# Moving a load of queries behind the first loop turn, and reordering the start, in an attention and ReGLU kernel

## The chip, the cores and the metric

The kernel runs on one core of a Trainium2 chip. The metric is the time of one execution on the device, in microseconds (us), given as the median of several executions with the lowest and the highest. The "span" of a profile is the time from the first to the last instruction of the profiled execution; here it is about 2 us shorter than the device time of the same execution. PE is TensorE, PEld its weight load, DVE is VectorE, ACT is ScalarE, POOL is GpSimd and SP is SyncE.

## The reference

```python
def _attn_ref(q, kv, w_sr):                       # q (4, 12288, 128), kv (4, 384, 32, 128)
    kv_pool = kv.reshape(B, H // 4, 4, W // 4, 4, C).mean(axis=(2, 4))
    k = v = kv_pool.reshape(B, -1, C) @ w_sr      # 768 keys of 128; keys and values are the same
    s = (q @ k.transpose(0, 2, 1)) / np.sqrt(C)
    a = np.exp(s - s.max(-1, keepdims=True))
    a /= a.sum(-1, keepdims=True) + 1e-09
    return a @ v

def _moe_ref(x, w_gate, w_val, w_out):            # x (49152, 128), weights 128 x 1536 and 1536 x 128
    return (np.maximum(x @ w_gate, 0.0) * (x @ w_val)) @ w_out
```

The output of the attention, seen as 49,152 rows, is the input of the second function. Input and output are in 32-bit floats; the kernel computes most matmuls in 16 bits.

## The kernel before

The kernel works on tiles of 512 query rows; four tiles are a group, whose queries are loaded and transposed together. One turn of the main loop has twelve steps. In each step TensorE does the value, gate and output projections of one 128-wide block of the feed-forward part for an earlier tile, and one twelfth of the attention of a later tile. Ahead of the loop stands a hand-ordered start: it loads the first image lines, pools and projects the 768 keys of the first batch, and does the attention of the first three tiles. All engines run in exactly the order in which the code issues instructions (`manual_schedule`), so moving a line in the source moves an instruction on its engine.

The parts that the change and the argument touch, with cuts marked:

```python
def q_load(g):                      # one group of queries: 512 KB of fp16, cast on the way, GpSimd's queue
    ...
    q16 = work.tile([128, GRP * NS, C], FP16, tag="q16", bufs=2)
    nc.gpsimd.dma_start(q16, q[b, n0 : n0 + GRP * T, :].rearrange("(p s) c -> p s c", p=128))

def q_turn(g):                      # its transposing DMA, on SyncE's queue
    ...
    nc.sync.dma_start_transpose(qT, q16.rearrange("p s c -> p (s c)"))

def block_move(kvT, blocks, i, j):  # 16 of these carry one pair of key chunks of a later batch
    rows, columns = slice(32 * i, 32 * (i + 1)), slice(32 * j, 32 * (j + 1))
    nc.sync.dma_start(kvT[columns, :, rows], blocks[rows, :, columns])
# ... cut ...
kv_load(0, 0, between=lambda: q_load_plain(0, 2))   # four image lines; queries after line 1
q_load_plain(2, GRP)
for pair in range(1, NJC // 2):
    kv_load(0, pair)                                # eight more image lines
# ... cut ...
def fill(n):                                        # matmuls that only keep TensorE's clock up
    for _ in range(n):
        nc.tensor.matmul(idle, ident16, filler, start=True, stop=True)
fill(8)
# ... cut: attention on image pairs 0 and 1 ...
scores_of(0, 1)
turn_values(0, 1)
s2 = add_lines(2)                                   # sum of two image lines, on VectorE
nc.vector.tensor_tensor(s2, s2, line(2, 2), op=ALU.add)
s1 = add_pixels(s2)
scores_of(1, 1)
# ... cut ...
gate = const.tile([128, 1], FP32)
nc.gpsimd.tensor_copy(gate, line(2, 2)[:, 0, 0, 0:1])   # holds GpSimd's loads back until line 2 is there
for own in (slice(0, D_FF // 2), slice(D_FF // 2, D_FF)):
    nc.gpsimd.dma_start(wv16[:, own], moe_w_val[:, own])
    nc.gpsimd.dma_start(wg16[:, own], moe_w_gate[:, own])
q_load(1)
q_turn(1)
nc.gpsimd.dma_start(wo16, moe_w_out.rearrange("(fb f) c -> f fb c", f=128))
q_load(2)
# ... cut: pair 2, the end of the start ...
for k in range(LAG, last + 1):
    g, ph = divmod(k, GRP)
    if ph == 1:
        q_turn(g + 1)
        q_load(g + 2)
    for step in range(NFB):
        # ... cut: out_proj(kO, step), value_proj(kF, step), scores or values of tile k, x_turn ...
        if kF < NT:
            gate_proj(kF, step)
```

The softmax here doesn't subtract the row's maximum and nothing guards it: scores larger than these inputs give would overflow.

## Time and profile before

| | before |
|---|---|
| device time, median of 3 (lowest to highest) | 1044.61 us (1044.28 to 1045.14) |
| span of the profile | 1042.5 us |
| TensorE busy | 1032.8 us, 99% |
| first value projection of the loop starts | 29.80 us |
| 14th value projection starts | 41.68 us |
| last value projection starts | 1035.48 us |

The page, the stretches and the chain of waits are shown in the prediction below.

### The profile page before, as it was taken

The page shows a single profiled execution, that of the slowest core. Times are in us where ns is not written, and L with a number is a line of the kernel's source. Part 1 is how long each engine was busy: PE and PEld are TensorE (multiplying, and loading weights), DVE is VectorE, ACT ScalarE, POOL GpSimd, SP SyncE. Part 2 cuts the span into 40 slices and gives each one's busy share as a digit, 9 for nine tenths or more (in the row PEclk, how much of TensorE's full clock was granted, in tenths as well). Part 3 has the DMA queues.
Part 4 walks back from the last instruction along what each step waited for, and adds up shares of the span by engine and source line. Part 5 has one row for each costly group of instructions (what it writes and reads, how often), then busy time and mean ns, then how long its engine had stood idle before and what let it go on. Part 6 is the DMA issues. An engine that isn't in the chain of part 4 may idle for free.

```text
span 1042.5 us, 26058 instructions
## 1 busy us (share of the span) xinstructions
PE 1032.8 (99%) x9928; PEld 684.6 (66%) x9928; DVE 911.9 (87%) x1669; ACT 909.5 (87%) x1749; POOL 107.0 (10%) x127
## 2 busy tenths in 40 slices
PE   8999999999999999999999999999999999999998
PEld 5566666666666666666666666666666666666665
DVE  3788889898988888998888888999888888888898
ACT  4888888888888888888888888888888888888887
POOL 2000045100000006400000003440000000000000
PEclk9999999999999999999999999999999999999999
DMA  8833254432322335534234134561531422212111
GB/s 300 129 76 76 78 178 137 96 76 52 87 53 66 72 124 141 150 79 80 61 58 87 31 87 132 150 159 41 92 80 39 73 63 55 67 31 67 32 47 47
DMA packets 140253, 92.53 MB, mean 89 GB/s; under 512 B 117728, under 2 KB 118624, under 8 KB 140128
## 3 DMA queue, kind: packets, MB, share of 16 engines
q1 hardware_dynamic: 134544, 77.56, 28.5%
q0 software_dynamic: 5440, 13.24, 7.7%
q8 instruction: 77, 1.26, 0.5%
q14 instruction: 48, 0.39, 0.1%
q10 hardware_dynamic: 144, 0.07, 0.0%
HBM read 52.76 MB, written 25.17 MB: 75 GB/s over the span
## 4 chain that ended last, share of the span: by engine, by line
PE 95%; DMA 4%; POOL 0%; SPq 0%; issue 0%; DVE 0%
PE bank_ps L285 25%; PE bank_ps L264 24%; PE bank_ps L275 24%; PE bank_ps L226 12%; PE bank_ps L215 11%; DMA parts<-in_kv_dram 2%; DMA qT<-q 1%; DMA q<-in_q_dram 1%; PE bank_ps L179 0%; DMA xT<-x 0%; SPq L128 0%; POOL wv L440 0%; POOL wg L441 0%; POOL gate L438 0%; SPq L93 0%
## 5 line engine op out<-in xcount | busy, mean ns | idle before, releaser
L278 DVE SCALAR_TENSOR_TENSOR hT<-bank_ps,val 128x512 f16<-128x512 f32 x1152 | 759.9, 686 | 101.2 <-ACT val L268 74.8
L268 ACT CAST val<-bank_ps 128x512 f16<-128x512 f32 x1152 | 677.9, 590 | 111.7 <-PE bank_ps L264 109.7
L285 PEld LDWEIGHTS <-hT 128*128 128x128 f16 x4608 | 353.2, 98 | 203.4 <-issue 0.2
L285 PE MATMUL bank_ps<-wo,hT 128*128 128x128 f16 x4608 | 443.6, 219 | 0.0
L264 PE MATMUL bank_ps<-xT,wv 128*128 128x512 f16 x1152 | 436.7, 379 | 0.2 <-DMA xT<-x 0.2
L275 PE MATMUL bank_ps<-xT,wg 128*128 128x512 f16 x1152 | 436.6, 379 | 0.0
L216 ACT ACTIVATE aT<-bank_ps 128x512 f16<-128x512 f32 x576 | 345.4, 604 | 1.4 <-PE bank_ps L215 1.3
L226 PE MATMUL bank_ps<-kv,aT 128*128 128x129 f16 x2304 | 223.5, 220 | 0.1
L226 PEld LDWEIGHTS <-aT 128*128 128x128 f16 x2304 | 177.2, 98 | 68.1 <-issue 0.6
L215 PE MATMUL bank_ps<-qT,kv 128*128 128x512 f16 x576 | 216.9, 379 | 2.6 <-DMA qT<-q 2.2
L275 PEld LDWEIGHTS <-wg 128*128 128x128 f16 x1152 | 112.7, 98 | 65.6
L264 PEld LDWEIGHTS <-wv 128*128 128x128 f16 x1152 | 112.7, 98 | 0.8 <-DMA xT<-x 0.4
L242 DVE TENSOR_TENSOR x<-bank_ps,rinv 128x256 f16<-128x256 f32 x188 | 79.7, 424 | 6.7
L78 POOL DMA_DIRECT2D q<-in_q_dram x23 | 12.5, 543 | 567.3 <-DMA qT<-q 567.2
L303 DVE TENSOR_SCALAR o_sb<-bank_ps 128x512 f32<-128x512 f32 (+1 forms) x95 | 64.0, 674 | 1.3 <-PE bank_ps L285 1.3
L139 POOL TENSOR_TENSOR s<-parts 128x512 f32<-128x512 f32 x36 | 45.3, 1269 | 163.4 <-DMA parts<-in_kv_dram 161.0
L215 PEld LDWEIGHTS <-kv 128*128 128x128 f16 x576 | 56.1, 98 | 5.2 <-DMA qT<-q 2.5
L234 DVE RECIPROCAL rinv<-bank_ps 128x2 f32<-128x2 f32 x192 | 30.6, 160 | 0.6 <-PE bank_ps L226 0.6
L141 POOL TENSOR_TENSOR s<-s 128x512 f32<-128x512 f32 x18 | 22.8, 1267 | 1.4
L143 POOL TENSOR_TENSOR c<-s 128x256 f32<-128x256 f32 x18 | 13.1, 726 | 1.4
L164 ACT COPY kvT<-bank_ps 128x128 f32<-128x128 f32 x4 | 1.1, 265 | 11.6 <-PE bank_ps L153 10.8
L146 POOL TENSOR_TENSOR kv_s<-c 128x128 f32<-128x128 f32 x18 | 8.2, 454 | 1.4
(46 smaller groups left out, 72.1 us busy)
## 6 DMA issues: line engine op xcount, KB each, us to landing
parts<-in_kv_dram SPq DMA_DIRECT2D x48, 512.0 KB, 6.5
out_dram<-o_sb SPq DMA_DIRECT2D x95, 256.0 KB, 2.1
q<-in_q_dram POOLq DMA_DIRECT2D x23, 512.0 KB, 5.2
kvT<-blocks SPq DMA_DIRECT2D x144, 8.0 KB, 1.8
xT<-x SPq DMA_TRANSPOSE x94, 2.5
q<-in_q_dram SPq DMA_DIRECT2D x2, 512.0 KB, 7.2
wv<-in_moe_w_val_dram POOLq DMA_DIRECT2D x2, 192.0 KB, 4.6
wg<-in_moe_w_gate_dram POOLq DMA_DIRECT2D x2, 192.0 KB, 5.0
```

Source lines behind the costliest of these rows:

```text
L139: eng.tensor_tensor(s2[:, i], parts[:, 2 * i, h], parts[:, 2 * i + 1, h], op=ALU.add)
L215: nc.tensor.matmul(s_ps, kv16[:, k // NST, jc, 0:C], qT_of(k), start=True, stop=True)
L216: nc.scalar.activation(aTs[k][:, jc, :], s_ps, AF.Exp, scale=qk_scale)
L226: nc.tensor.matmul(x_ps[:, i, :], aTs[k][:, jc, s * 128 : (s + 1) * 128], kv16[:, k // NST, jc, C : 2 * C + 1], start=(jc == 0 and i == 0) ...
L234: nc.vector.reciprocal(rinvs[k, half], x_banks[k, half][:, :, C : C + 1])
L242: nc.vector.tensor_tensor(x16s[k][:, 2 * half : 2 * half + 2, :], x_ps[:, :, 0:C], rinv.to_broadcast([128, 2, C]), op=ALU.mult,)
L264: nc.tensor.matmul(va_ps, wv16[:, fb * 128 : (fb + 1) * 128], xTs[k], start=True, stop=True)
L268: nc.scalar.copy(val, va_ps)
L275: nc.tensor.matmul(g_ps, wg16[:, fb * 128 : (fb + 1) * 128], xTs[k], start=True, stop=True)
L278: nc.vector.scalar_tensor_tensor(hTs[k][:, fb, :], g_ps, 0.0, vals.pop((k, fb)), op0=ALU.max, op1=ALU.mult)
L285: nc.tensor.matmul(o_ps, hTs[k][:, fb, s * 128 : (s + 1) * 128], wo16[:, fb, :], start=first, stop=(fb == NFB - 1), skip_group_check=True,)
L303: nc.vector.tensor_scalar(o_sb, o_ps, 1.0 / X_SCALE**2, None, op0=ALU.mult)
```

## The change

The intent is a shorter start. The load of the third group of queries (`q_load(2)`) leaves the place where it runs beside the transposing DMA of the second group, and goes behind the last activation of the first loop turn. The first queries are loaded behind the whole first image pair. The cast of the second tile's queries goes to ScalarE, so that two casts run side by side. The scores of three tiles come before the values' transposes of pair 1, the sum of the lines of pair 2 moves ahead of them, and four fillers go.

```diff
-    def q_cast(i):
+    def q_cast(i, engine=nc.vector):
         q16 = work.tile([128, NS, C], FP16, tag="q16s", bufs=3, name="q16s")
-        nc.vector.tensor_copy(q16, q32s[i])
+        if engine is nc.scalar:
+            nc.scalar.copy(q16, q32s[i])
+        else:
+            nc.vector.tensor_copy(q16, q32s[i])
 ... cut: kv_load loses its argument "between" ...
-    kv_load(0, 0, between=lambda: q_load_plain(0, 2))
-    q_load_plain(2, GRP)
+    kv_load(0, 0)
+    for i in range(0, GRP, 2):
+        q_load_plain(i, i + 2)
 ...
-    for i in range(2):
-        q_cast(i)
     for dh in range(3):
         for h in range(2):
             turn_add(h, line(0, dh, h), first=dh == 0)
-        if dh == 1:
-            fill(3)
-            q_turn_pe(0)
-            q_turn_pe(1)
-            fill(1)
 ...
         project_chunk(h, (nc.vector, nc.scalar)[h])
+    for i in range(2):
+        q_cast(i, (nc.vector, nc.scalar)[i])
+        q_turn_pe(i)
+    scores_of(0, 0)
+    scores_of(1, 0)
     for i in range(2, GRP):
         q_cast(i)
-    scores_of(0, 0)
-    scores_of(1, 0)
     q_turn_pe(2)
+    turn_values(0, 0)
     q_turn_pe(3)
-    turn_values(0, 0)
 ...
-    scores_of(0, 1)
+    s2 = add_lines(2)
+    for k in range(GRP - 1):
+        scores_of(k, 1)
     turn_values(0, 1)
-    s2 = add_lines(2)
     nc.vector.tensor_tensor(s2, s2, line(2, 2), op=ALU.add)
     s1 = add_pixels(s2)
-    scores_of(1, 1)
-    scores(2, 2)
     attend(0, 1)
-    scores(2, 3)
     scores_of(3, 1)
 ...
     nc.gpsimd.dma_start(wo16, moe_w_out.rearrange("(fb f) c -> f fb c", f=128))
-    q_load(2)
 ...
                 gate_proj(kF, step)
+            if k == LAG and step == NFB - 1:
+                nc.gpsimd.tensor_copy(gate, hTs[kF][:, step, 0:1])
+                q_load(2)
```

The source lines shift by the change: line 264 (value projection) becomes 265, 215 (scores) 216, 275 (gate projection) 276, 268 (value cast on ScalarE) 269, 216 (exponential) 217, and GpSimd's gate copy goes from 438 to 434.

More of the change, by code (lines that the diff above doesn't have):

```diff
@@ L120, with kv_load @@
     kv_in = {}
-    def kv_load(b, pair, between=None):
+    def kv_load(b, pair):
         parts = work.tile([128, r, 2, r, C], FP32, tag="kv_in", bufs=3)
@@ L128, in kv_load @@
             nc.sync.dma_start(parts[:, dh].rearrange("p h dw c -> p (h dw c)"), rows[dh])
-            if dh == 1 and between is not None:
-                between()
         kv_in[b, pair] = parts
```

## The prediction

> **What bounds the kernel now.** I read the page first: busy time per engine, then the busy tenths by slice.
>
> ```profile
> PE 1032.8 (99%) x9928; PEld 684.6 (66%) x9928; DVE 911.9 (87%) x1669; ACT 909.5 (87%) x1749; POOL 107.0 (10%) x127
> PE   8999999999999999999999999999999999999998
> ```
>
> The reader is to see that TensorE is the bound for the whole span and that only 1042.5 - 1032.8 = 9.7 us of it are idle. The change takes no matmul out of the loop, so it can only win part of these 9.7 us, and 2% would be 20.9 us. Next I asked for the busy time by stretches, to find where the idle time lies (columns: stretch, length, busy time of PE, PEld, DVE, ACT and POOL with counts, granted clock, DMA share, GB/s):
>
> ```profile
> 5.35:13.00 7.65, 6.78 (x49) 4.80 (x49) 2.16 (x7) 0.27 (x1) 0.00 (x0) 1.00 1.02 386
> 13.00:20.00 7.00, 6.82 (x60) 5.09 (x59) 3.39 (x7) 5.20 (x13) 0.00 (x0) 1.00 1.03 412
> 20.00:30.00 10.00, 9.03 (x78) 5.79 (x78) 5.82 (x14) 7.30 (x16) 5.24 (x8) 1.00 0.78 147
> 30.00:40.00 10.00, 8.83 (x76) 5.33 (x74) 9.02 (x20) 9.79 (x24) 0.00 (x0) 1.00 1.29 193
> 40.00:50.00 10.00, 8.99 (x78) 5.57 (x79) 7.15 (x12) 8.59 (x18) 0.53 (x1) 1.00 0.48 72
> 80.00:1030.00 950.00, 949.82 (x9193) 630.70 (x9192) 849.41 (x1550) 843.27 (x1614) 99.38 (x109) 1.00 0.35 83
> ```
>
> From 80 to 1030 us PE is idle for 0.18 us; the rest of the idle time is in the first 42 us and the last 3.6. The largest single hole is around 40 us. The chain of waits, in order of time (start, length, what), says what it is made of:
>
> ```profile
> 11.06 10.21 DMA parts<-in_kv_dram
> 24.43 8.23 DMA q<-in_q_dram
> 32.67 0.02 issue
> 32.68 8.28 DMA qT<-q
> 40.97 0.05 issue
> 41.01 0.39 PE bank_ps L215
> ```
>
> Two things to see. Until about 22.8 us the start follows the image lines as they land back to back (about 1.27 us per 512 KB at some 410 GB/s). Then the second group of queries (q of group 1) lands at 32.67, its transposing DMA lands at 40.97, and PE starts at once. On the timeline the preceding value projection starts at 38.45, so the score matmul was due at 38.45 + 0.22 = 38.67: the hole costs 41.01 - 38.67 = 2.34 us. Last, what ScalarE does around that hole (timeline: start, length, engine, operation, idle before):
>
> ```profile
> 39.02 0.66 ACT L240 ACTIVATE x<-bank_ps,rinv 128x128 f16<-128x128 f32 x2
> 39.53 0.62 ACT L268 CAST val<-bank_ps 128x512 f16<-128x512 f32 x1
> 41.44 0.60 ACT L216 ACTIVATE aT<-bank_ps 128x512 f16<-128x512 f32 x1 [1.28 <-PE bank_ps L215]
> ```
>
> ScalarE comes out of the first loop turn late: it works until 40.15 on what PE finished by 38.8, and is idle for only 1.28 us of the hole.
>
> **What the Trainium skill says.** "DMA: Bandwidth & Descriptors", section "Issuing engines are not separate DMA queues": DMAs of the scalar, sync and gpsimd engines end on the same 16 DMA engines and interleave. The trace agrees: this transpose, beside the loads of wo (lands 34.85) and of the third group (issued 25.97, lands 12.4 us later at 38.37), takes 8.28 us; the same transpose for group 2, at 51.3 us beside one 256 KB store, takes 4.4 us. "TensorE: Matmul & The Clock Gate", Part 1 (The HAM clock gate) has a half clock until the array has been busy for about 3.4 us, and Part 4 (PE-mode transpose) says that transposes do not count as busy in the same way. The trace shows the start: eight fillers take 3.59 us (about 0.43 us each) at 1.7 us, later 128x512 matmuls follow every 0.22 us. Whether the four later fillers keep the clock up is what no run here shows yet. "ScalarE: Activation LUTs", What ACT_TABLE_LOAD costs, gives an ACTIVATE with immediate operands 186 ns + 0.833 ns per column, 613 ns for 512; the trace has 604 for the exponentials.
>
> **The change part by part.**
>
> 1. *Third group's load moved.* Its issue goes from 25.97 us to behind the last activation of the first loop turn (about 40.2 us). So it is gone from the DMA engines while the group 1 transpose runs. Rate under contention: 8.28 us were 5.69 us contended (32.68 to 38.37) plus 2.59 alone; against 4.4 alone that leaves (4.4 - 2.59) / 5.69 = 0.32 of full speed while contended. After the change only wo contends, to 34.85: 2.17 us x 0.32 = 0.69 us of work, the other 3.71 alone, landing at about 32.67 + 2.17 + 3.71 = 38.6, just when PE wants it (38.67). The DMA part of the hole, 2.34 us, should be nearly gone. I do not expect q of group 1 itself to land earlier, since it is ahead of the third group on its queue.
>
> 2. *What ScalarE gives back.* Without the hole ScalarE still has its backlog to 40.02, so its first exponential of this turn moves from 41.44 to 40.02 at best: 1.42 us. In this turn its two steps take 1.52 us (exponentials start at 44.76 and 46.28) and PE's two steps 1.53 (score matmuls at 44.08, 45.60), so it catches up nothing until the next turn, where it first idles (0.19 us every two steps from 52.1). PE can be ahead of it only as far as 8 PSUM banks let it. With a lag of about 1.3 us a value bank is held 1.9 us every 0.76, a score bank 1.9 every 1.53, a gate bank some 2.3 every 0.76, an output bank always: 2.5 + 1.2 + 3.0 + 1 = 7.7 banks, at the edge. I take 1.9 us, between 1.42 (PE fully tied) and 2.34 (not at all).
>
> 3. *First queries behind the whole first image pair.* In the old order image lines 2 and 3 land at 9.78 and 11.04, queries at 8.27 and 12.33. In the new one the lines should land at about 7.9 and 9.3 and the first queries at 11.0. Keys are then ready at about 11.3, but cast, transposes and copy (0.42 + 0.35 + 0.42 with hand-overs) put the first scores at about 12.5 instead of 13.00. That half microsecond ends at the next image lines, which land as before (17.46 for the last of pair 1; the total of bytes ahead is the same): worth about 0.1 us.
>
> 4. *Second cast on ScalarE.* Some 0.5 us (estimated between the 0.42 of DVE and the 0.59 of a value cast) on an engine that waits there: L164 of ScalarE idles 9.6 us before 12.2. It lets two casts run side by side; contained in the 12.5 above.
>
> 5. *Scores of three tiles before the values' turn of pair 1, line sum first.* The 1.22 us sum for pair 2 moves ahead, to 20.0 us. But six score matmuls now stand ahead of the values' transposes; four banks are free, so these wait for the third exponential (20.17 + 3 x 0.51 = 21.7), DVE copies at 22.1 instead of 20.79, and the two sums that follow end at about 24.3 instead of 24.19. PE's transposes of the last line come after eight value matmuls and two scores, at 23.4 instead of 22.9. The serial chain from there to the loop (24.25 to 29.80) moves by about +0.2 us.
>
> 6. *Four fillers gone*: 4 x 0.22 = 0.88 us, all in time when PE waits for lines: 0.
>
> Sum: -1.9 - 0.1 + 0.2 = -1.8 us, plus +0.1 for the clock risk below (20% of a delay, of which the later waits hide most): 1044.6 - 1.7 = **1042.9 us**.
>
> **The rivals.**
>
> *ScalarE takes the place of the DMA.* The hole goes, but PE stalls for banks shortly after. For: ScalarE 9.79 busy of 10 us from 30 to 40, and 5.00 of 5 from 45 to 50. Against: PE ran through the first turn with a lag of 1.1 us. Time: about 1043.2.
>
> *The transpose stays late.* If wo, with its small rows, was the one that slowed it, it lands near 39.5 to 40 and the gain is 1 us or less: 1043.7. For: the transpose and wo overlap from the first moment. Against: the third group overlaps 3.5 us more.
>
> *The clock falls.* From 5.3 to 12.5 us PE now runs nothing but transposes and two small projections. If it drops to half speed, eight scores, the transposes and values before pair 1 take about 2.5 us more than their 3.3, which pushes the start by 1 to 2 us: 1043.5 to 1045. Against: the old stretch had only 4 fillers in 7.6 us and the image lines, not PE, set the pace to 22.8.
>
> *The start gets faster.* If lines land 0.4 us sooner (DMA moved only 320 GB/s in the 6 to 8 us slice, where the queries cut in), all follows: 1042.3.
>
> **Range and chances.** The sure part is 1 to 1.4 us, the full hole plus a better start 2.9. Run to run spread is 0.9 us. So 8 in 10 for 1041.5 to 1044.5. Neither side comes near 20.9 us: 0.98 for within 2%, 0.01 each for the others.
>
> **What would show it.** Step 1 right: the transpose of group 1 takes under 6.5 us and PE's wait for it is under 0.3 us. Step 2 right: ScalarE has no idle of 1 us at 40 us, and PE has waits on ACT or DVE of 0.2 to 0.8 us between 39 and 55. Step 3: first score near 12.5 and pair 1's last line still near 17.5. Step 5: first value projection between 29.6 and 30.2. The clock: score matmuls at 12.5 to 15 us longer than 0.38 us, or spaced 0.43, would show the fall. I would be wrong above all if a new hole of over 1 us appears before 30 us, or if the third group, now issued at the same time as the fourth, delays the transposes behind it on the sync queue so that PE waits at 50 or 60 us.

## More of the kernel before

The value projections are good marks, since each step has one of them: the first shows when the loop starts, the distance from the first to the 14th shows what the first turn and the step after it cost, and the rest is the steady loop. One more view of the kernel before is worth having, TensorE's waits (engine, tile and line, what it waited for, then us in total, times, longest):

```profile
PE bank_ps L215 <- DMA qT<-q: 2.2, 1, 2.2
```

It is the largest wait of TensorE in the whole kernel. The line says that a score matmul (line 215) waited once, for 2.2 us, for the transposed queries.

## The result and the profile after

| | before | after |
|---|---|---|
| device time, median of 6 (lowest to highest) | 1044.88 us (1044.15 to 1046.53) | 1042.90 us (1041.60 to 1043.41) |
| ratio of the means, 95% interval | | 0.9978 (0.9965 to 0.9991) |
| span of the profile | 1042.5 us | 1041.0 us |
| first value projection | 29.80 us | 30.07 us |
| from the first to the 14th | 11.88 us | 9.61 us |
| from the 14th to the last | 993.80 us | 994.33 us |

The change is within 2%, and the median is the one predicted. The last three rows say where the time went: the loop starts 0.27 us later, the first turn is 2.27 us shorter, and 0.53 us is lost later in the loop. The last value projection comes 1.47 us earlier (1035.48 and 1034.01), which is the difference of the spans.

The first line of the page after, busy time by engine:

```profile
PE 1032.3 (99%) x9924; PEld 684.2 (66%) x9924; DVE 911.7 (88%) x1668; ACT 909.8 (87%) x1750; POOL 106.6 (10%) x128
```

Four matmuls fewer are the four fillers; one instruction more on ScalarE is the moved cast, and one more on GpSimd the new gate copy. TensorE's idle time in the span is now 1041.0 - 1032.3 = 8.7 us. The stretches after, with the columns that the prediction explains:

```profile
5.35:13.00 7.65, 6.03 (x45) 4.60 (x46) 1.34 (x4) 1.05 (x3) 0.00 (x0) 1.00 0.97 359
20.00:30.00 10.00, 8.84 (x77) 5.76 (x77) 5.59 (x13) 7.33 (x16) 3.96 (x7) 1.00 0.94 189
30.00:40.00 10.00, 9.94 (x85) 6.08 (x84) 8.97 (x22) 9.52 (x24) 0.00 (x0) 1.00 0.80 118
40.00:50.00 10.00, 10.00 (x90) 6.23 (x89) 8.98 (x15) 10.00 (x21) 1.26 (x3) 1.00 0.67 120
80.00:1030.00 950.00, 949.62 (x9190) 630.22 (x9189) 849.35 (x1551) 843.30 (x1614) 99.53 (x109) 1.00 0.34 83
```

The two rows from 30 to 50 us carry the gain: TensorE was busy for 8.83 and 8.99 us of them before, and is for 9.94 and 10.00 now. The 40 to 50 row has ScalarE busy for all of its 10.00 us and TensorE busy for all of its 10.00 us as well: ScalarE is full, and TensorE does not wait for it. TensorE's timeline around the old hole (start, length, engine, line, operation):

```profile
38.73 0.38 PE L265 MATMUL bank_ps<-xT,wv 128*128 128x512 f16 x1
39.00 0.38 PE L216 MATMUL bank_ps<-qT,kv 128*128 128x512 f16 x1
39.24 0.38 PE L276 MATMUL bank_ps<-xT,wg 128*128 128x512 f16 x1
```

The score matmul that had to wait until 41.01 follows the value projection by 0.27 us. The second group's transposing DMA was issued at 31.92 and landed at 37.92, in 6.00 us where it had taken 8.28. The chain of waits after, up to the start of the loop:

```profile
12.33 11.20 DMA parts<-in_kv_dram
23.67 1.50 PE bank_ps L154 x12
...
29.59 0.44 DVE xT L260
30.07 0.38 PE bank_ps L265
```

The transposing DMA has left the chain. What now leads into the loop is the last image line, then TensorE's transposes of it (line 154) and the chain behind them. In the largest waits of TensorE after, the queries are gone as well, and the image lines have taken the first place among the loads:

```profile
PE bank_ps L154 <- DMA parts<-in_kv_dram: 1.3, 3, 0.6
...
PE bank_ps L265 <- DMA xT<-x: 0.2, 1, 0.2
```

Finally ScalarE's timeline in the first and second loop turns, after:

```profile
39.82 0.63 ACT L269 CAST val<-bank_ps 128x512 f16<-128x512 f32 x1
40.28 0.66 ACT L217 ACTIVATE aT<-bank_ps 128x512 f16<-128x512 f32 x1
...
41.71 0.69 ACT L217 ACTIVATE aT<-bank_ps 128x512 f16<-128x512 f32 x1
...
43.15 0.72 ACT L217 ACTIVATE aT<-bank_ps 128x512 f16<-128x512 f32 x1
```

And the same engine before, after its hole:

```profile
43.23 0.60 ACT L216 ACTIVATE aT<-bank_ps 128x512 f16<-128x512 f32 x1
...
44.76 0.60 ACT L216 ACTIVATE aT<-bank_ps 128x512 f16<-128x512 f32 x1
```

Exponentials come once in two steps. Before, they came 44.76 - 43.23 = 1.53 us apart, after 43.15 - 41.71 = 1.44. With work waiting for it, ScalarE does two steps in 1.44 us; TensorE needs 1.53. So it catches up about 0.1 us in every two steps, and the 1.53 of before was TensorE's pace and not ScalarE's.

### The profile page after: what moved, and what is told of

Its sections match the earlier page's. It is cut to its first block, busy times and chain, and to the rows that moved or that the text cites. A ratio compares the mean times of both kernels' runs of the same rounds, so it can differ in the third digit from the quotient of the medians.

```text
span 1041.0 us, 26051 instructions
## 1 busy us (share of the span) xinstructions
PE 1032.3 (99%) x9924; PEld 684.2 (66%) x9924; DVE 911.7 (88%) x1668; ACT 909.8 (87%) x1750; POOL 106.6 (10%) x128
## 4 chain that ended last, share of the span: by engine, by line
PE 96%; DMA 3%; SPq 0%; ACT 0%; issue 0%; DVE 0%
PE bank_ps L286 25%; PE bank_ps L265 24%; PE bank_ps L276 24%; PE bank_ps L227 12%; PE bank_ps L216 11%; DMA parts<-in_kv_dram 1%; DMA q<-in_q_dram 1%; DMA xT<-x 1%; PE bank_ps L180 0%; SPq L131 0%; ACT aT L217 0%; PE bank_ps L154 0%; PE bank_ps L172 0%; SPq L93 0%; PE bank_ps L258 0%
## 5 line engine op out<-in xcount | busy, mean ns | idle before, releaser
L78 POOL DMA_DIRECT2D q<-in_q_dram x23 | 12.5, 544 | 550.2 <-DMA qT<-q 549.8
```

## The experiments

The theory was that one thing carries the gain: the third group's load no longer runs beside the transposing DMA of the second group, which lands in time (theory 1). The rivals were that another part carries it, that ScalarE or the clock gives something back, and that the load of the output weights wo is what slows the transposing DMA. Twelve runs were made, all with correct results; e10 repeats the changed kernel and e12 repeats e4. In the table, "landed" is the last image line, "first" is the start of the first value projection, "13 steps" the distance from it to the 14th, "rest" from the 14th to the last, all in us and from one profiled execution each.

| run | landed | first | transposing DMA | 13 steps | rest | time, median us | ratio to before (95%) |
|---|---|---|---|---|---|---|---|
| before | 22.77 | 29.80 | 8.28 | 11.88 | 993.80 | 1044.88 | |
| after | 23.53 | 30.07 | 6.00 | 9.61 | 994.33 | 1042.90 | 0.9978 (0.9965 to 0.9991) |
| e1_load_only | 23.92 | 30.45 | 4.56 | 9.61 | 994.67 | 1043.48 | 0.9985 (0.9968 to 1.0003) |
| e2_rest_only | 23.70 | 30.23 | 7.86 | 10.73 | 994.65 | 1044.32 | 0.9991 (0.9973 to 1.0008) |
| e3_sum_first | 23.32 | 29.89 | 7.41 | 10.63 | 994.08 | 1044.83 | 1.0003 (0.9977 to 1.0028) |
| e4_values_early | 23.48 | 30.05 | 5.42 | 9.61 | 993.32 | 1043.59 | 0.9986 (0.9968 to 1.0004) |
| e5_no_fillers | 22.56 | 30.75 | 4.72 | 9.61 | 994.23 | 1043.64, one run | |
| e6_seven_banks | 23.62 | 30.56 | 6.16 | 9.86 | 994.67 | 1044.10, one run | |
| e7_ten_copies | 23.64 | 30.18 | 5.57 | 11.71 | 994.36 | 1045.37, one run | |
| e8_wo_first | 23.89 | 30.44 | 4.39 | 9.78 | 993.36 | 1042.65, one run | |
| e9_moves_split | 23.36 | 29.89 | 6.04 | 9.60 | 1000.57 | 1046.60 | 1.0024 (0.9995 to 1.0053) |
| e10_changed_again | 23.36 | 29.90 | 6.03 | 9.59 | 995.26 | 1043.27 | 0.9992 (0.9980 to 1.0004) |
| e11_moves_spread | 23.64 | 30.17 | 5.62 | 9.61 | 1043.78 | 1093.63 | 1.0476 (1.0462 to 1.0491) |
| e12_values_early_again | 23.52 | 30.05 | 5.97 | 9.61 | 993.33 | 1042.58 | 0.9987 (0.9975 to 1.0000) |

The "rest" column is the warning that goes with the table: for kernels whose loops hold the same instructions it lies anywhere from 993.3 to 995.3, so a single profile can be 2 us long or short for reasons outside the start. The times decide less than the traces do here. The whole effect is about 2 us of 1044. The runs of one kernel mostly spread by 1 to 3 us, but those of the kernel before in the rounds of e1 to e4 by 5.5 us (1043.11 to 1048.58). Apart from the slow e11, only the main comparison has an interval that leaves out 1; what each part does is read from the marks.

### e1_load_only: the load's move alone

```diff
 (before)
-    q_load(2)                      # behind the load of wo
...
+            if k == LAG and step == NFB - 1:
+                nc.gpsimd.tensor_copy(gate, hTs[kF][:, step, 0:1])
+                q_load(2)
```

> The kernel before with one edit: the third group's load goes behind the last activation of the first loop turn, nothing else. Theory A (the hole at 40 us came from the third group's load on the DMA engines): the first value projection stays at 29.80 us, the second group still lands near 32.7, its transpose takes 5.8 to 6.3 us instead of 8.28, PE waits 0 to 0.4 us instead of 2.2, and at 50 us the kernel is 2.0 to 2.3 us ahead of before; time about 2.0 us under before. Rival B (the hole closed because the second group's own load was issued 0.73 us earlier in the changed kernel): the transpose still ends after 39.5 us, PE waits over 0.8 us, and the time is less than 1.5 us under before.

TensorE's timeline of this run at the old hole:

```profile
39.12 0.38 PE L264 MATMUL bank_ps<-xT,wv 128*128 128x512 f16 x1
39.39 0.38 PE L215 MATMUL bank_ps<-qT,kv 128*128 128x512 f16 x1
```

The score matmul follows the value projection by 0.27 us, as in the changed kernel, and the 13 steps take 9.61 us, to the hundredth what they take there. So this one part removes the whole hole. The transposing DMA landed at 37.84 although it was issued at 33.28, 0.60 us later than before. The start came 0.65 us later than before's, because in this execution the last image line landed 1.15 us later, which the edit can't have caused: nothing ahead of it was touched.

### e2_rest_only: all parts but the load's move

```diff
 (after)
     nc.gpsimd.dma_start(wo16, ...)
+    q_load(2)
...
-            if k == LAG and step == NFB - 1:
-                nc.gpsimd.tensor_copy(gate, hTs[kF][:, step, 0:1])
-                q_load(2)
```

> The changed kernel with the third group's load put back where it stood. Theory A: first value projection at 30.07 us as in the changed kernel, second group lands near 31.9, its transpose takes about 8.3 us again and ends near 40.2; PE waits about 1.0 to 1.3 us; at 50 us 0.6 to 1.1 us ahead of before. Rival B (the earlier issue alone closes the hole): PE waits under 0.4 us and the kernel is as fast as the changed one.

The chain of waits of this run:

```profile
23.89 8.48 DMA q<-in_q_dram
...
32.39 7.86 DMA qT<-q
```

And TensorE's timeline:

```profile
40.30 0.39 PE L216 MATMUL bank_ps<-qT,kv 128*128 128x512 f16 x1 [1.02 <-DMA qT<-q]
```

With the third group back in its old place the transposing DMA takes 7.86 us, and TensorE waits for it again, 1.02 us. The hole is smaller than before's 2.18 us for two reasons: the transposed queries landed 0.72 us earlier (40.25 instead of 40.97; the queries had been issued at 23.89 instead of 24.43, and e7 below shows where that comes from), and the loop itself came 0.43 us later. Theory 1 stands: the move of the load is needed for the gain, and by e1 it is enough for it.

### e3_sum_first: only the sum's order

```diff
 (before)
+    s2 = add_lines(2)
     scores_of(0, 1)
     turn_values(0, 1)
-    s2 = add_lines(2)
```

> The kernel before with one edit: VectorE's first line sum of the third image pair stands ahead of the scores of pair 1 and so ahead of the copy of the values. Theory C (the 0.94 us of the one-element copy on GpSimd was a wait for VectorE's 1.22 us sum of two SBUF operands, which ended at 22.21, just before the copy ended at 22.26): the sum now runs at 20.0 to 21.3, the copy takes about 0.2 us, the weights' loads start near 21.45 instead of 22.20, and the second group lands near 31.9. Rival D (the copy's length has nothing to do with VectorE): it stays at 0.9 us. The start should also come 0.2 to 0.4 us sooner (value projection at 29.4 to 29.6), and the hole at 40 us should shrink by some 0.4 us only, since PE is there sooner too; the time about 0.7 us under before.

The ratio is 1.0003, so this part alone has no effect that the times show. The gate copy on GpSimd took 0.19 us instead of 0.94, as expected, but the run does not test the reason: image line 2 of pair 2 landed only at 22.23 here, and the sum had ended by then (21.56). For the same cause the loads were not issued earlier (queries at 24.65), and the earlier start that was expected (29.4 to 29.6) did not come: the last line landed at 23.32 and the loop started at 29.89. The transposing DMA took 7.41 us and TensorE waited 0.9 us for it.

### e4_values_early and e12_values_early_again: the values' transposes back behind the first scores

```diff
 (after)
-    for k in range(GRP - 1):
-        scores_of(k, 1)
-    turn_values(0, 1)
+    scores_of(0, 1)
+    turn_values(0, 1)
+    for k in range(1, GRP - 1):
+        scores_of(k, 1)
```

> The changed kernel with the values' transposes of pair 1 back behind the first tile's scores (the line sum stays first). Theory E (the 0.27 us that the changed kernel's start is later comes from the six score matmuls ahead of these transposes, which wait for banks): the copy of the values runs near 21.3 us instead of 22.05, PE takes the last image line near 22.9 instead of 23.67, and the first value projection comes at 29.4 to 29.7 instead of 30.07; no hole at 40 us as long as the transpose ends by 38.4; time 0.3 to 0.6 us under the changed kernel. Rival F (the lateness comes from the queries behind the image pair): it stays at 30.07.

> The version with the values early once more, without the spreading, beside it on the same chip. Theory E again: if the line before last lands near 21.3 us this time, VectorE's sums end near 23.3 to 23.6 instead of 24.2, and the first value projection comes 6.5 us after the last line; if that line is late again (past 22.2), the start is bound by it and is no earlier than in the changed kernel. Step from the first to the fourteenth value projection 9.55 to 9.7 us; loop stalls anything from 0 to 1.7 us, so a span of 1039.5 to 1041.5.

The question was whether the new order of pair 1 costs the start something, as the prediction's step 5 had it. The loop started at 30.05 us in both runs and at 30.07 in the changed kernel, so with the last line landing this late it does not. The reason stands in the column "landed": from the last line's landing to the first value projection it is 6.53 to 6.57 us in the changed kernel and in all of e1 to e4 and e7 to e12, whichever order pair 1 has. In the second run the VectorE sums ended at 23.83, 0.37 us earlier than the changed kernel's 24.20, and the loop started no earlier for it. What the order costs when the last line lands as early as before (22.77) no run shows. Both profiles are short (spans of 1039.9 and 1040.0 us), but through the "rest" column. The ratios, 0.9986 and 0.9987, lie between the changed kernel's own two, 0.9978 and 0.9992. I can't call this version better.

### e5_no_fillers: is it the fillers that raise the clock?

```diff
 (after)
-    fill(8)
+    fill(0)
```

> The changed kernel without the eight fillers at the start either, so that TensorE does only transposes and two projections before the first scores near 12.5 to 13 us. Theory G (transposes do not wake the clock, so fillers matter): the first 128x512 score matmuls last about 0.6 us and follow every 0.43 us, and the first value projection is 0.5 to 2 us later than 30.07. Rival H (any work wakes it, or the wait for lines hides it): score matmuls of 0.38 us and the first value projection within 0.3 us of 6.5 us after the last image line lands.

TensorE's timeline of this run, its first group of transposes and its first scores:

```profile
5.30 6.56 PE L154 MATMUL bank_ps<-ident,parts 128*128 128x128 f32 x32 [5.30 <-DMA parts<-in_kv_dram]
...
13.93 1.16 PE L216 MATMUL bank_ps<-qT,kv 128*128 128x512 f16 x4
```

The prediction feared that a stretch of nothing but transposes lets the clock fall. Here the kernel has no fillers at all. Within the first group the starts of the transposes are 0.21 us apart for the first 27 of them, some 5.8 us, and 0.11 us apart from then on. The scores at 13.93 are 0.38 us long and 0.21 to 0.22 apart, which is the full pace. So transposes alone raised the clock, after about 5.9 us, and in the changed kernel, where eight fillers had raised it, they kept it up: its transposes from 5.32 on and its scores from 12.99 on have the full pace too. The first scores came 0.94 us later than in the changed kernel, and the loop started 0.68 us later (30.75). In this run the lines had landed early (22.56), so TensorE's lag and not the line set the start. This is one execution, but it speaks for keeping the eight fillers; the four others were not missed. One thing to know for reading: the granted clock of the profile says 1.00 in this stretch, so here it is the spacing that shows the slow pace and not that column (in e11 below the column does show it).

### e6_seven_banks: are eight PSUM banks the limit beside ScalarE?

```diff
 (after)
-psum = ctx.enter_context(tc.tile_pool(name="psum", bufs=8, space=bass.MemoryType.PSUM))
+psum = ctx.enter_context(tc.tile_pool(name="psum", bufs=7, space=bass.MemoryType.PSUM))
```

> The changed kernel with 7 PSUM banks instead of 8. The prediction counted 7.7 banks in use while ScalarE is behind, from 39 to 50 us, and so a loss for want of banks. Theory I (banks are at the edge there): with 7, PE stalls between 39 and 50 us by 0.5 to 2 us in sum and the step from the first value projection to the fourteenth is 10 us or more instead of 9.61. Rival J (the count was too high, ScalarE's lag shrinks by itself): that step stays within 0.3 us of 9.61. In either case the start can be later, since scores wait for banks there.

A PSUM bank is one of the eight buffers of this program into which TensorE writes its results; it is free again when ScalarE or VectorE has read it. The prediction counted 7.7 banks in use in the turn with ScalarE behind, and gave back 0.44 us for it. With a bank less the step from the 13th to the 14th value projection took 0.92 us, in the changed kernel 0.95, and the eleven steps after it 8.29 us, before 8.28. There is no wait for a bank in that turn even with seven. The run lost 0.25 us, in the turn before (9.86 against 9.61), and its loop started 6.94 us after the last line instead of 6.53 to 6.57. It is not a test at the lag that the prediction assumed: with TensorE that much later, the first exponential behind the old hole was only 1.04 us behind its score matmul, against 1.28 us in the changed kernel. There the lag shrinks at each score, 1.28, 1.16, 1.06, 0.97, to 0.69 at the seventh. The prediction held it at 1.3 us.

### e7_ten_copies: hold the queries back through the copies' own time

```diff
 (after)
     nc.gpsimd.tensor_copy(gate, line(2, 2)[:, 0, 0, 0:1])
+    for _ in range(10):
+        nc.gpsimd.tensor_copy(gate, line(2, 2)[:, 0, 0, 0:1])
```

> The changed kernel with ten more one-element copies on GpSimd behind the one that opens the weights' loads. Theory C (a GpSimd copy waits for a VectorE sum of two SBUF operands): copies that start while no such sum runs take 0.19 us; one that meets VectorE's sum takes 0.5 to 1.3 us and ends with it. Rival D: all eleven take about 0.19 us. The weights and the second group are issued 1 to 2.5 us later, so its transpose ends near 39 to 40.5 us and the hole at 40 us comes back with 0.3 to 1.5 us: it also measures how the hole follows the time of issue.

This answers a surprise in the two main traces. Image line 2 of pair 2 landed at 21.27 in both, but the queries were issued at 24.43 before and at 23.70 after. GpSimd's timeline of before shows the gate copy that stands ahead of the loads:

```profile
21.32 0.94 POOL L438 COPY gate<-parts 128x1 f32<-128x1 f32 x1 [19.30 <-DMA parts<-in_kv_dram]
```

VectorE's timeline of before, the sum of two lines:

```profile
20.99 1.22 DVE L377 TENSOR_TENSOR kv_s<-parts 128x1024 f32<-128x1024 f32 x1
```

The copy started at 21.32 during the sum, and ended at 22.26 just after the sum did (22.21). After, the sum runs from 20.10 to 21.33, and the same copy is short, on GpSimd's timeline of after:

```profile
21.33 0.19 POOL L434 COPY gate<-parts 128x1 f32<-128x1 f32 x1 [19.30 <-DMA parts<-in_kv_dram]
```

In this run, GpSimd's timeline has the ten copies as one group:

```profile
21.59 3.79 POOL L436 COPY gate<-parts 128x1 f32<-128x1 f32 x10
```

Taken singly, one of them ran from 22.33 to 23.43 and one from 23.49 to 24.16; all others took 0.19 us. VectorE's timeline has its two sums here:

```profile
22.18 1.22 DVE L428 TENSOR_TENSOR kv_s<-kv_s,parts 128x1024 f32<-128x1024 f32 x1
23.42 0.69 DVE L385 TENSOR_TENSOR kv_s<-kv_s 128x512 f32<-128x512 f32 x1
```

Each long copy began inside a sum and ended within 0.04 us of its end. This is what the Trainium skill states in "SBUF — State Buffer", section "Who interferes with whom": a VectorE instruction with two inputs in SBUF contends with a GpSimd instruction that reads SBUF. The trace agrees: a copy of 0.19 us took 0.94 us before, and 1.10 and 0.67 us here. So moving the line sum ahead, which was meant for VectorE, brought GpSimd's loads forward by 0.73 us. The delay of 3.86 us (queries issued at 27.56 instead of 23.70) also shows what the queries' issue is worth without the third group in the way: the score matmul waited 1.67 us (0.3 to 1.5 was expected), and the 13 steps took 11.71 us.

### e8_wo_first: the transposing DMA alone

```diff
 (after)
+    nc.gpsimd.dma_start(wo16, ...)
     q_load(1)
     q_turn(1)
-    nc.gpsimd.dma_start(wo16, ...)
```

> The changed kernel with the output weights loaded ahead of the second group instead of behind it, so that nothing but the transpose is on the DMA engines when it runs. By the contention reckoning of the prediction the transpose takes 4.4 us alone (5.96 in the changed kernel beside the output weights). The second group lands about 2.2 us later, near 34.1 to 35, the transpose ends near 38.5 to 39.4, PE waits 0 to 0.5 us. If the transpose takes 5.5 us or more, the output weights were not what it lost time to.

The chain of waits of this run:

```profile
26.22 8.89 DMA q<-in_q_dram
...
35.12 4.38 DMA qT<-q
```

With nothing beside it, the transposing DMA takes 4.38 us, which is what it takes in the loop (median 4.3). This gives the scale: alone 4.4 us; beside wo 4.6 to 6.2 (e1, e4 to e7, e9 to e12 and the changed kernel); beside wo and the third group 7.4 to 8.3 (before, e2, e3). The third group is the larger part, and wo matters little: in e1 wo landed at 36.10, 2.8 us into the transposing DMA, which still took only 4.56.

The packets of these traces say more than the sums do. Beside the third group, the transposing DMA's first packet came 3.13 us (before), 2.64 (e2) and 3.33 (e3) after its issue; in all runs without it, beside wo or alone, 1.3 us. So 1.83 of the 2.28 us between before and after are a later first packet and not a slower transfer; why it comes later stays open. What is left between 4.4 and 6.2 us goes with fetches of instructions, 16 KB each on one DMA engine. In the seven runs where one began while the packets of the transposing DMA moved (the changed kernel, e4, e6, e9 to e12), it took 5.4 to 6.2 us; in e1, e5 and e8, where it began before the first packet or after the last, 4.4 to 4.7. e7, with 5.57 us, lies between: its fetch began 0.06 us before the first packet. Before, e2 and e3 had such a fetch in their midst too. In the changed kernel 15 of the 16 parts in which a landing is reported were in 4.44 us after the issue, and the last came 1.56 us later. No experiment isolates the fetch. The order of e8 gains nothing, since the queries land 3.2 us later (35.11 against 31.90) and the transposing DMA at 39.51 is just late (9.78 against 9.61).

### e9_moves_split, e10_changed_again and e11_moves_spread: the half microsecond lost in the loop

In the loop of the changed kernel the matmuls' starts show gaps (beyond what the columns of the matmul before take, counted above 0.1 us) of 0.87 us in all, before 0.35. They sit near 185, 439 and 715 us, where the 16 block moves of a key pair occupy SyncE's queue for 10.6 to 12.8 us, longer than a loop turn of 10.45 us, and the transposing DMAs of the next tile stand behind them. The theory was that this queue is the cause. e10 is the changed kernel once more, unaltered. e9 and e11 start from e4; e9 puts half of the moves on GpSimd's queue, e11 spreads them over two turns.

```diff
 (e9, from e4)
-        nc.sync.dma_start(kvT[columns, :, rows], blocks[rows, :, columns])
+        queue = nc.sync if j % 2 else nc.gpsimd
+        queue.dma_start(kvT[columns, :, rows], blocks[rows, :, columns])
```

```diff
 (e11, from e4)
-                    if not odd and 2 <= step < 10:
-                        for _ in range(2):
-                            block_move(*moves.pop())
+                    if (step < 8) if odd else (step >= 4):
+                        block_move(*moves.pop())
```

> The best version so far (values early, third group late) with half of the later images' block moves issued by GpSimd instead of the sync queue. In the loop PE lost 0.35 us before, 0.87 in the changed kernel, 1.25, 1.23 and 0.68 in three experiments and 0.00 in the fourth, each time near 185, 440 or 715 us, where 16 block moves hold up the sync queue for 11 to 13 us. Theory K (this queue is what delays the transposes of x and the keys): no stall over 0.1 us in the loop, span 1039.5 to 1040.3, time 0.5 to 1.5 us under the changed kernel and 2 to 3 under before. Rival L (the GpSimd queue, held by its pixel sums and query loads, delays the moves): stalls of 0.5 us or more at the projections of later images.

> The changed kernel itself once more, to see what varies between executions. Theory: the span is the sum of three parts: the start (first value projection about 6.5 us after the last image line has landed, and that line varies by up to 1.2 us with the time of a 16 KB instruction fetch near 20 us), no hole at 40 us (first to fourteenth value projection in 9.6 us), and the loop's stalls of 0 to 1.3 us. So: first value projection 29.6 to 30.6, step 9.55 to 9.7, span within 1040 to 1042; time 1042 to 1043.5. Rival: the start is the changed order's own and stays at 30.07 whatever the lines do.

> The version with the values early and the third group late, with the later images' 16 block moves still on the sync queue but one per step over two turns instead of two per step in one. Theory K (moves bunched on the sync queue for 11 to 13 us, more than a turn of 10.45 us, hold up the transposes behind them): the loop's stalls fall to 0.4 us or less in sum, against 0 to 1.7 us in the six executions with bunched moves seen so far; span 1039.5 to 1040.5; time 0.5 to 1.2 us under the changed kernel's 1042.9 to 1043.3. Rival M (the stalls come from contention on the DMA engines, not from the queue's order): 0.5 us or more remain.

e10 has gaps of 1.68 us where the same kernel had 0.87, and e4, e8 and e12, whose loops hold the same instructions, have none above 0.1 us. So the 0.53 us of the main comparison is scatter from one execution to the next and not a cost of the change. The cure failed twice. In e9 the gaps grew to 6.4 us and the times spread from 1042.21 to 1051.68 us; the waits of its TensorE name the transposes of the tiles again (line 266 is the value projection there):

```profile
PE bank_ps L266 <- DMA xT<-x: 3.9, 2, 2.2
```

In e11 my own edit was at fault. The moves end two steps before the projection that needs them, and the last ones landed near 190 us, 4.8 us after their issue. TensorE's timeline:

```profile
183.44 0.38 PE L276 MATMUL bank_ps<-xT,wg 128*128 128x512 f16 x1
190.20 1.19 PE L180 MATMUL bank_ps<-kvT,w_sr_f 128*128 128x256 f32 x2 [6.38 <-DMA kvT<-blocks]
...
191.61 0.63 PE L265 MATMUL bank_ps<-xT,wv 128*128 128x512 f16 x1
...
195.86 0.38 PE L276 MATMUL bank_ps<-xT,wg 128*128 128x512 f16 x1
```

TensorE waited 6.38 us, and then its matmuls were 0.63 us long and 0.43 us apart for more than 5 us, half the usual pace, until 195.5 (the profile's granted clock says 0.50 there). TensorE waited 35.9 us for these moves in all, in 7 waits, and the clock came on top: the kernel is 4.8% slower. This is the clock that the prediction took from "TensorE: Matmul & The Clock Gate", Part 1, now shown inside a loop. What makes the gaps in the loop differ from run to run stays open; neither edit removed them, and neither was clean enough to drop the queue as their cause.

## Why the prediction was right, point by point

**The hole (step 1): the cause is right and shown, the reckoning is not.** The prediction had the transposing DMA at 5.9 us (2.17 contended and 3.71 alone) and measured were 6.00; alone it had 4.4, and e8 gave 4.38. But its rule, 0.32 of full speed beside wo, would give 6.3 us for e1 and 6.1 for e5, which took 4.56 and 4.72 (wo landed 2.82 and 2.43 us into them). That 5.9 fits the changed kernel is luck: what is over 4.44 us there is the last of 16 parts, late beside a fetch of instructions (e8). The prediction also did not expect the second group to land earlier; it landed at 31.90 instead of 32.67 (e7), which gave the transposing DMA 0.77 us to spare. e1 does without that and still has no hole. The prediction set under 6.5 us and a wait under 0.3 us as the test; the waits are gone. e1 and e2 show that the load's move alone does it. The rival in which wo slows the transposing DMA as much as the third group fell with e1 and e8.

**What ScalarE gives back (step 2): the mis-sized term of the sum.** The prediction took 1.9 us of the 2.34, for fear of waits for PSUM banks. The 13 steps became 2.27 us shorter, and TensorE had no such wait from 40 to 50 us. The step that failed was the sentence "In this turn its two steps take 1.52 us": it read the spacing of ScalarE's exponentials as ScalarE's own pace, while ScalarE was fed at TensorE's pace. When work is queued for it, it needs 1.44 us for two steps. The forecast of waits on ScalarE or VectorE of 0.2 to 0.8 us between 39 and 55 us was wrong: there are none with eight banks, nor with seven (e6, at a smaller lag).

**First queries behind the first pair (step 3) and the second cast (step 4): no gain in the main comparison.** The first scores came at 12.99 us, before at 13.00; 12.5 was expected. The image lines that were to land at 7.9 and 9.3 landed at 8.24 and 9.79, and the cast on ScalarE took 0.61 us instead of 0.5. Over two more runs with the same order the first scores came at 12.40 (e4) and 13.41 (e12), so the place moves with the landing of the loads by more than the expected gain. That this is worth nothing later was right: the last line of pair 1 landed at 17.44, before at 17.45.

**The start (step 5): the right number for the wrong reason.** +0.2 us was expected, from the order of TensorE's queue, and +0.27 measured. The sums ended at 24.20 as expected (24.3). But what set the start was the last image line, 23.53 instead of 22.77, and e4 and e12 show that the order makes no difference to it when that line lands this late. In the kernel before the line had landed early enough for the sums to be the last, which ended at 24.19; from there to the first value projection it was 5.61 us. The late landing has a visible companion: at 20.86 us (before at 19.83) one DMA engine fetched 16 KB of instructions for 1.0 to 1.1 us, in the midst of the last image lines, and between 22 and 23 us the engines moved only 18 GB/s while the line was still not complete. That the fetch delays the line is argued from these packets; no experiment isolated it.

**Fillers and clock: right that their removal costs nothing.** The extra 0.1 us for the risk was not needed, and e5 shows why: transposes hold the clock, and even raise it.

**The sum.** The prediction had -1.9 - 0.1 + 0.2 + 0.1 = -1.7 us. The traces have -2.27 for the hole, +0.27 for the start, and +0.53 of scatter in the loop, which is -1.47. The medians moved by 1.98 us, and the second run of the changed kernel shows a gain of 0.08% of about 1044 us, 0.8 us, with an interval that includes none at all. That the median came out at the predicted 1042.9 is therefore partly luck: a gain in the hole that was 0.4 us larger than expected was offset by a loop that happened to be slower. What is shown is the size of the hole that went and its cause.

## What to carry to other kernels

When a wait for a transfer stands in the chain, look first at which other transfers share its time: here a load had landed at 38.37 us for a use at 51.30, and moving it out of the way took 2.3 us from another transfer, for which TensorE waited. Do not read an engine's pace from its spacing while another engine feeds it; look for a stretch in which work is queued for it. When the gain is 0.2%, let the marks in the traces decide (where the loop starts, how long the first turn takes), and run the same kernel twice to learn what scatters by itself.

## What the Trainium skill lacked or had wrong

- No page tells that fetches of instructions can hold up the kernel's own transfers; "Runtime: NRT & Kernel Launch", section "Instruction fetch mechanics", has their 16 KiB blocks, a DMA queue for them and a cost that is mostly hidden. Here a fetch of 16 KB took one engine for 1.0 to 1.1 us in the midst of the image lines. The last line landed anywhere from 22.56 to 23.92 us in fourteen traces, while 15 of its 16 parts were always there by 22.07 to 22.96. That one causes the other is argued and not isolated.
- "TensorE: Matmul & The Clock Gate", Part 4 (PE-mode transpose), says that transposes do not count as busy in the same way, and that the full clock does not engage for them. In e5, with nothing but (32-bit) transposes, their spacing went from 0.21 to 0.11 us after about 5.9 us, and the scores behind them had the full pace. In that one execution it took longer than the 3.59 us of the eight fillers of the other runs.
- "DMA: Bandwidth & Descriptors", section "Latency and other measured facts", has about 350 to 400 GB/s for a contiguous transposing DMA, and 261 for one with a non-contiguous middle dimension. Here 512 KB (524,288 bytes) alone took 4.38 us from issue to landing, 120 GB/s; by the difference to the 128 KB transposes of the loop (medians 4.3 and 2.5 us, 393,216 bytes in 1.8 us) it is, by estimate, some 220 GB/s without the fixed part. No page tells what it takes beside other loads: up to 8.3 us here, with the first packet 2.6 to 3.3 us after the issue instead of 1.3.
- The same page, section "Issuing engines are not separate DMA queues", says that issuing from several engines saves only the time of issuing. It does not say that it can also lose: in e9, with half of the block moves on GpSimd's queue, the gaps in the loop were 6.4 us in the one profile, against 0 to 1.7 in the kernels with all of them on SyncE's in the same bunches. What made them was not found.
